# Adding the halves of y in the store, two queues for the last results, and a later place for two loads

## The chip, the cores and the metric

The kernel runs on one core of a Trainium2 chip. What counts is the device time of one execution in microseconds (us); the text compares medians of several runs. The core has five engines that work side by side: TensorE (PE in the rows, its weight loads PEld), VectorE (DVE), ScalarE (ACT), GpSimd (POOL) and SyncE (SP). SP, ACT and POOL can each issue DMA transfers; every one of them issues in the order of its own instructions, so an issue that waits holds up what stands behind it on that engine.

## What is computed

Local attention (chunks of 32 queries over 64 keys) gives x of 3072 x 512. Two gated blocks without activation follow:

```python
a = x @ w1 ; b = x @ w2            # 512 -> 1024
y = ((a * b) @ w3) @ w_out         # 1024 -> 1024 -> 512
a = y @ w_a ; b = y @ w_b          # 512 -> 1536
out = (a * b) @ w_out2             # 1536 -> 512
```

All is float32; the kernel splits every float32 operand into a high and a low part and makes a product from three matrix multiplications.

## The kernel before

The tokens are cut into six blocks of 512 (`t` = 0 to 5, `TT` = 512, `NT1` = 6). The first four go through the first gated block one by one while attention still runs. Blocks 4 and 5 go through it as one pair, with seven block products in place of eight (`seven12`); all three pairs go through the second gated block that way (`seven`). One call of `seven` makes one of 12 gate blocks (`f` = 0 to 11) from 42 matrix multiplications of 512 columns. The loop over pairs is called a stage here: first stage (`si` = 0, blocks 0 and 1), second (`si` = 1, blocks 2 and 3), third (`si` = 2, blocks 4 and 5).

**The pair's y.** For blocks 4 and 5 the sum over the 1024 inner columns is made in two halves (`h` = 0, 1). In each half eight results (`groups`, 128 x 512 each) are copied from PSUM by ACT (`copied`, L1041) into a buffer `tmp` of eight, and SP stores them in HBM, the first half to `yh`, the second to `yd` (L1169). `y_sums` adds the two much later: in the second stage it loads both (L851), DVE adds them (L1479), and SP stores the sum to `yd` (L1480). `x_sums` then makes the differences of the next pair's y that the seven products want (`xm`).

**Weights of the gate blocks.** POOL loads each gate block's factors in two DMAs (`w7_a` L920 with 640 KB, `w7_b` L939 with 256 KB) into two buffers in turn. ACT makes their high parts (`w7_hi`, L107), DVE the low parts (L110), between the copies and sums that `seven` does for PE. The factors used in call `f` are loaded in call `f` - 2 and split in call `f` - 1.

**Where the first stage begins**, several things meet: the last stores of y, the raw output weights of the last two blocks `j` = 4, 5 (`o_late`: four DMAs of 512 KB into the region of `gh`, L1390), and the first factors of the output products (`fo_load`: 768 KB each, L1209). `o_late` is a generator whose steps `hooks` calls at fixed places (`f`, `n`) of the loop; `n` counts four points inside one `seven`.

**Results.** `out_put` subtracts or adds on DVE (L1363), transposes on DVE (L1364), and issues four stores of 64 KB per piece on SP (L1367). `owed` holds four `out_put` calls of a stage that are done in the next stage at places (`f`, `n`).

Of the kernel before, what the change touches and what calls it, by code (L numbers as in the profile page):

```python
# [11 lines left out]
ALU = mybir.AluOpType  # L12

P = 128
# [9 lines left out]
TT = 512  # L24
# [23 lines left out]
def tile_attention_moe(  # L48
# [32 lines left out]
    def dram_tile(n, shape):  # L81
        return dram.tile(shape, F32, name=n, tag=n)

    yd = [dram_tile(f"yd{i}", [P, KD, TT]) for i in range(NT1)]
    yh = {i: dram_tile(f"yh{i}", [P, KD, TT]) for i in range(ND, NT1)}
    xd = {i: dram_tile(f"xd{i}", [P, KD, TT]) for i in range(ND, NT1)}

    W7 = 7 * CH // 2
# [1034 lines left out]
    for t in range(ND, NT1, 2):  # L1123
        for h in range(2):
            gs = {}
            held[:] = [psx.tile([P, 512], F32, tag="x", name="ps7")[:, :TT] for _ in range(2)]
            for m in range(HM * h, HM * h + HM):
                gs[m] = g_new(2 * (m % HM)), g_new(2 * (m % HM) + 1)
                if m == M1 - 1:
                    xn = []  # L1130
                    xg = x_build(xn, xd, t + 2) if t + 2 < NT1 else x_build(xn, yd, 0)
                    next(xg)
                seven12(m, w7.pop(0), *gs[m])
            if h == 1:
                while fo_rest:
                    fo_lo[0]()
                xn.extend(x_new() for _ in range(8))
                fo_hi[:] = [xn[7].rearrange("p l k t -> p (l k) t")]
            groups = [(n, i) for n in range(KD) for i in range(2)]
            ps_of = {}  # L1140

            def y_some(j, m0, m1):
                n, i = groups[j]
                if j not in ps_of:
                    ps_of[j] = psd.tile([P, 512], F32, tag="d", name="psY")
                for m in range(HM * h + m0, HM * h + m1):
                    for k, (a, b) in enumerate(PASSES):
                        mm(
                            ps_of[j][:, :TT],
                            wsm[m][:, a, P * n : P * n + P],  # L1150
                            gs[m][i][:, b, :],
                            m % HM == 0 and k == 0,
                            m % HM == HM - 1 and k == 2,
                        )

            for j, (n, i) in enumerate(groups):
                if j == 0:
                    y_some(0, 0, HM - 1)
                    sixth()
                    g_split()  # L1160
                    if h == 1:
                        w7_split(2)
                        w7_ab()
                    y_some(1, 0, HM - 1)
                    y_some(2, 0, HM - 1)
                y_some(j, HM - 1 if j < 3 else 0, HM)
                ps = ps_of.pop(j)[:, :TT]
                z = copied(ps)
                nc.sync.dma_start(out=(yd if h else yh)[t + i][:, n, :], in_=z)  # L1169
                if h == 1:  # L1170
                    for _ in range(2 + (j > 0)):
                        next(xg, None)
                    hook(4)
                else:
                    hook()
        for _ in xg:
            pass
        xs = xn
# [174 lines left out]
    def out_new(pool, tag):  # L1353
        return [pool.tile([P, 512], F32, tag=tag, name="ops") for _ in range(2)]

    def out_put(ps, y, op, t, n, banks=(0, 1), dst=None):
        for b in banks:
            if dst is None:
                sb = tmp()
                ob = cp.tile([P, TT], F32, tag="ob", bufs=3, name="ob")  # L1360
            else:
                sb, ob = gated(0, HF + dst + b), gated(1, HF + dst + b)
            nc.vector.tensor_tensor(sb, ps[b], y[b], op)  # L1363
            nc.vector.transpose(ob, sb)  # L1364
            for i in range(4):
                c0 = HC * n + P * b + SQ * i
                (nc.sync, nc.sync, nc.sync, nc.sync)[i].dma_start(  # L1367
                    out=out[t * TT : t * TT + TT, c0 : c0 + SQ].rearrange("(s p) c -> p s c", p=SQ),
                    in_=ob[SQ * i : SQ * i + SQ].rearrange("p (s c) -> p s c", c=SQ),
                )  # L1370

    def kept(ps, z):
        for b in range(2):
            nc.scalar.activation(z[b], ps[b], AF.Copy)
        return z

    def chain(*gs):
        for g in gs:
            yield from g

    def o_late():
        n = CH // 2
# [44 lines left out]
                nc.vector.tensor_tensor(x, x, e.bitcast(F32), ALU.subtract)  # L1427
                store(j, k, 1, x)

        for j in js[:2]:  # L1430
            for i in range(2):
                load(j, i)
        yield
        for j in js:
            for i in range(2):
                for _ in conv(j, i):
                    yield
            if j + 2 < HF:
                for i in range(2):
                    load(j + 2, i)  # L1440
            a, b = ((0, 2), (6, 8))[j - JE]
            sums[j] = [u[:, a + i // 2, n * (i % 2) : n * (i % 2) + n] for i in range(4)]
            s2 = [u[:, a + i] for i in range(2)]
            free[:] = [b, b + 1] + free[:2]
            for x in ((0, 1), (2, 3)):
                for i in x:
                    add(j, i)
                yield
            for k, x in ((0, decs[j, 0]), (2, s2[0]), (4, s2[1]), (6, decs[j, 1][:, :n])):
                hi(j, k, x)  # L1450
                yield
                lo()
# [3 lines left out]
    def room(i):  # L1456
        return [spare[:, 2 * i + b] for b in range(2)]

    def y_sums():
        todo = [(n, i) for n in range(KD) for i in range(ND, NT1)]  # L1460
        pend = []

        def load():
            if todo:
                n, i = todo.pop(0)
                k = 2 * (len(todo) % 2)
                x, y = spare[:, k], spare[:, k + 1]
                y_load(x, yd, i, n)
                y_load(y, yh, i, n)
                pend.append((n, i, x, y))  # L1470

        load()
        yield
        while pend:
            load()
            for _ in range(4):
                yield
            n, i, x, y = pend.pop(0)
            nc.vector.tensor_tensor(x, x, y, ALU.add)  # L1479
            nc.sync.dma_start(out=yd[i][:, n, :], in_=x)  # L1480
            yield

    def other(n):
        for _ in range(n):
            next(cw, None)
# [3 lines left out]
    for si, t in enumerate(seq):  # L1489
        nxt = seq[si + 1] if si + 1 < len(seq) else None  # L1490
        if si == 0:
            spare = spare_of(xs.pop())
            cw = x_sums(nxt)
            ow = o_late() if JE < HF else iter(())
            next(ow, None)
        elif si == 1:
            cw = chain(y_sums(), x_sums(nxt))
        order = (B11, T1, T2, B22, T3) if nxt is not None or not 1 else (B11, T1, T2, T3, B22)
        todo = [(i, j) for i in order for j in range(HF)]
        pd = pb = None  # L1500
        for f in range(M2):
            j = f - HF
            if si == 0 and f in (2, 3, 7, 8):
                fo_load(1, nc.sync)

            def hooks(n):
                if n == 0 and j >= 0:
                    put(T4, j, nc.vector)
                    put(B21, j, nc.vector)
                if owed and (f, n) in ((0, 1), (0, 2), (0, 3), (1, 0), (1, 1), (1, 2)):  # L1510
                    out_put(*owed.pop(0))
                if n > 0 and f == M2 - 1:
                    for _ in range((0, 1, 2, 2)[n]):
                        put(*todo.pop(0), nc.vector)
                if si == 0:
                    for _ in range((1, 0, 1, 2)[n] if f in (1, 2, 3, 4, 5) else 0):
                        next(ow, None)
                other((1, 0, 1, 1)[n] * (f >= 6) if si == 0 else (2 * (f > 0), 0, 2, 1)[n])

            if si == 0 and f == HF:  # L1520
                for _ in ow:
                    pass
            seven(w7.pop(0), gated(0, f), gated(1, f), hooks)
            if j >= 0:
                if j == 0:
                    pd, pb = out_new(pso, "o"), out_new(pso, "o")
                out_part(t, pd, T4, j, True)
                s_sum(1, j)
                s_sum(3, j)
                out_part(t, pb, B21, j, True)  # L1530
# [9 lines left out]
        for i in order:  # L1540
# [13 lines left out]
                    out_part(t, ps, i, j, i in (B11, T1))  # L1554
                step += 1
            if final and i == B22:
                out_put(pa, p4, ALU.subtract, t, 0, dst=2)
                out_put(pa, s5, ALU.add, t, 1, dst=4)
            if final:
                for b in range(2):  # L1560
                    for j in range(HF):
                        out_part(t, ps, i, j, False, (b,), b == 1)
                    if i == B22:
                        out_put(pc, u2, ALU.add, t + 1, 1, (b,))
                        continue
                    out_put(pa, p4, ALU.subtract, t, 0, (b,))
                    out_put(pa, s5, ALU.add, t, 1, (b,))
# [103 lines left out]
```

## Time and profile before

| What | us |
|---|---|
| median of 3 runs (1037.01 to 1041.54) | 1040.45 |
| the profiled execution, its own time | 1042.75 |
| its span in the trace | 1040.9 |
| PE busy | 1023.6 (98%) |
| DVE busy | 733.4 (70%) |
| ACT busy | 491.2 (47%) |
| POOL busy | 155.3 (15%) |

The profiled execution took 1.85 us more than its span, and it was longer than each of the three runs. Busy PE is not PE at its best, since matrix multiplications overlap and since the granted clock can be below full speed. All times in the rows below count from the span's start.

### The profile page before, as it was taken

What the parts mean: (1) busy time and instruction counts of PE and PEld (TensorE: products, weight loads), DVE (VectorE), ACT (ScalarE), POOL (GpSimd) and SP (SyncE); (2) the same over time, 40 slices, a digit from 0 to 9 for tenths busy, and PEclk for the clock granted to TensorE, in tenths of its full rate; (3) what the DMA queues carried; (4) which work ended last, traced back from release to release, by engine and by line L of the source; (5) the groups of instructions that cost most, each with busy time, mean ns of one, the idle gap of its engine ahead of it and who ended that gap; (6) DMA issues with size and microseconds to landing.
All of it is one profiled execution on the core that took longest, in us unless ns stands there. A gap on an engine that the chain in (4) does not pass through costs nothing.

```text
span 1040.9 us, 18743 instructions
## 1 busy us (share of the span) xinstructions
PE 1023.6 (98%) x7294; PEld 816.9 (78%) x7294; DVE 733.4 (70%) x1166; ACT 491.2 (47%) x883; POOL 155.3 (15%) x204
## 2 busy tenths in 40 slices
PE   9899999999999999999999999999999999999996
PEld 3458888888888888888878888877888888888885
DVE  4888936666665356768767778986677996666694
ACT  5676613444443345465545335643433653343342
POOL 0111497122232000001001000001011000100000
PEclk9999999999999999999999999999999999999999
DMA  8886567768886434577645774987538787223174
GB/s 330 295 238 195 156 205 241 236 230 275 276 298 190 133 106 162 175 271 230 220 155 180 244 246 145 315 238 201 184 118 273 258 304 189 91 87 132 36 219 104
DMA packets 147800, 212.95 MB, mean 205 GB/s; under 512 B 60544, under 2 KB 101376, under 8 KB 146432
## 3 DMA queue, kind: packets, MB, share of 16 engines
q1 hardware_dynamic: 137104, 170.30, 50.6%
q0 software_dynamic: 9856, 40.38, 12.0%
q8 instruction: 57, 0.93, 0.4%
q10 hardware_dynamic: 752, 1.09, 0.3%
q14 instruction: 31, 0.25, 0.1%
HBM read 159.29 MB, written 52.43 MB: 203 GB/s over the span
## 4 chain that ended last, share of the span: by engine, by line
PE 41%; DVE 5%; issue 4%; DMA 3%; ACT 1%; SPq 0%; DVEq 0%; POOLq 0%; ACTq 0%
PE ps L1029 28%; PE ops L1327 12%; DMA w<-wc 2%; DVE wo L1218 1%; DMA x<-yh 1%; DVE w L110 0%; DVE x L110 0%; DVE tmp L1278 0%; DMA x<-yd 0%; DVE ob L1364 0%; DVE gl L1349 0%; DVE tmp L1363 0%; DVE tmp L1045 0%; ACT wo L107 0%; DVE gh L1363 0%
## 5 line engine op out<-in xcount | busy, mean ns | idle before, releaser
L1029 PE MATMUL ps<-x,w 128*128 128x512 f32 x1848 | 427.1, 391 | 4.0 <-ACT tmp L1041 2.4
L1029 PEld LDWEIGHTS ps<-x,w 128*128 128x128 f32 x1848 | 346.4, 188 | 81.4 <-ACT tmp L1041 3.9
L1041 ACT ACTIVATE tmp<-ps 128x512 f32<-128x512 f32 x132 | 78.6, 595 | 248.8 <-PE ps L1029 195.8
L1327 PE MATMUL ops<-wo,fo 128*128 128x512 f32 x756 | 174.9, 390 | 0.2 <-DVE wo L1218 0.2
L1327 PEld LDWEIGHTS ops<-wo,fo 128*128 128x128 f32 x756 | 141.7, 188 | 30.5 <-DVE wo L1218 0.8
L110 DVE TENSOR_TENSOR w<-w 128x512 fp32r<-128x512 f32 (+1 forms) x176 | 105.5, 619 | 42.8 <-ACT w L107 42.7
L97 PE MATMUL psY<-g,wo 128*128 128x512 f32 x576 | 134.5, 392 | 0.0
L97 PEld LDWEIGHTS psY<-g,wo 128*128 128x128 f32 x576 | 107.4, 188 | 22.3
L1278 DVE TENSOR_TENSOR tmp<-ps,tmp 128x512 f32<-128x512 f32 x108 | 74.2, 687 | 33.2 <-PE ps L1029 30.6
L97 PE MATMUL psA<-xt,w 128*128 128x512 f32 x384 | 94.4, 395 | 0.5 <-ACT xt L107 0.5
L107 ACT ACTIVATE w<-w 128x512 fp32r<-128x512 f32 (+1 forms) x176 | 92.1, 571 | 3.8 <-DMA w<-wc 3.8
L97 PE MATMUL psB<-xt,w 128*128 128x512 f32 x384 | 93.8, 393 | 0.0
L97 PEld LDWEIGHTS psA<-xt,w 128*128 128x128 f32 x384 | 70.8, 188 | 15.7 <-ACT xt L107 0.9
L97 PEld LDWEIGHTS psB<-xt,w 128*128 128x128 f32 x384 | 71.2, 188 | 14.9
L920 POOL DMA_DIRECT2D w<-wc x36 | 19.3, 536 | 418.1 <-PE ps L1029 177.2
L1218 DVE TENSOR_TENSOR wo<-gl,wo 128x512 fp32r<-128x512 f32 x90 | 59.7, 686 | 28.8 <-ACT wo L107 28.8
L412 ACT ACTIVATE raw<-raw 128x512 f32<-128x512 f32 (+1 forms) x62 | 46.2, 745 | 32.1 <-DMA raw<-in_wab 17.5
L107 ACT ACTIVATE wo<-gl 128x512 fp32r<-128x512 f32 x90 | 52.9, 626 | 9.3 <-PE ops L1327 8.9
L97 PE MATMUL wps<-w_f 128*128 128x512 f32 x112 | 50.3, 599 | 0.6 <-DVE w_f L418 0.6
L413 ACT ACTIVATE raw<-raw 128x512 uint32<-128x512 uint32 (+1 forms) x62 | 46.2, 745 | 0.0
L762 DVE TENSOR_TENSOR gv<-psB,gv 128x512 f32<-128x512 f32 x32 | 22.0, 687 | 28.1 <-PE psB L97 24.4
L97 PEld LDWEIGHTS wps<-w_f 128*128 128x128 f32 x112 | 20.6, 190 | 25.6 <-issue 21.3
(103 smaller groups left out, 1010.0 us busy)
## 6 DMA issues: line engine op xcount, KB each, us to landing
fo<-fo SPq DMA_DIRECT2D x42, 768.0 KB
w<-wc POOLq DMA_DIRECT2D x36, 640.0 KB, 4.4
raw<-in_wab SPq DMA_DIRECT2D x24, 512.0 KB
v<-in_vw SPq DMA_DIRECT2D x64, 168.0 KB
w<-wc POOLq DMA_DIRECT2D x36, 256.0 KB, 4.7
kraw<-in_kt SPq DMA_DIRECT2D x16, 512.0 KB
raw<-in_w3a SPq DMA_DIRECT2D x6, 1024.0 KB
q<-in_qt SPq DMA_DIRECT2D x16, 384.0 KB
```

The costliest lines, as they stand in the source:

```text
L97: nc.tensor.matmul(o, lhsT=l, rhs=r, start=first, stop=last)
L107: nc.scalar.activation(hi, src, AF.Copy)
L110: nc.vector.tensor_tensor(lo, src, hi.bitcast(F32), ALU.subtract)
L412: nc.scalar.activation(h, h, AF.Prelu, scale=2.0**-112, alpha=2.0**32)
L413: nc.scalar.activation(l, l, AF.Copy, scale=2.0**-29)
L762: nc.vector.tensor_tensor(gv, psB[:, :TT], gv, ALU.mult)
L920: nc.gpsimd.dma_start(out=t[:, 1, :C7].bitcast(F32), in_=wseq[n][:, :C7])
L1029: nc.tensor.matmul(ps, lhsT=w[i][:, a, k, :], rhs=xs[i][:, b, k, :], start=first and n == 0, stop=n == 5, skip_group_check=not first,)
L1041: nc.scalar.activation(z, ps, AF.Copy)
L1218: low.tensor_tensor(e[:, 1, :n], src, e[:, 0, :n].bitcast(F32), ALU.subtract)
L1278: nc.vector.tensor_tensor(z, ps, y, ALU.add)
L1327: nc.tensor.matmul(ps[s], lhsT=w[:, b, P * s : P * s + P], rhs=e[:, a, :], start=fresh and j == 0 and n == 0, stop=j == HF - 1 and n == 2, ...
```

## The change

Five edits. The second half of y is no longer stored by SP to an array of its own: POOL stores it with addition onto the first half, and `yh` and `y_sums` are gone. `x_sums` of the second stage starts at `f` = 5 alone. `o_late` asks for the raw weights of `j` = 5 after it has converted those of `j` = 4, and the first two `fo_load` move from `f` = 2, 3 to `f` = 3, 5. The four `owed` results go to places (0,1), (0,3), (1,1), (1,3). The stores of the last stage's results are dealt to SP and ACT in turn (`late`).

```diff
-    yh = {i: dram_tile(f"yh{i}", [P, KD, TT]) for i in range(ND, NT1)}
...
-                nc.sync.dma_start(out=(yd if h else yh)[t + i][:, n, :], in_=z)
+                if h == 0:
+                    nc.sync.dma_start(out=yd[t + i][:, n, :], in_=z)
+                else:
+                    nc.gpsimd.dma_start(out=yd[t + i][:, n, :], in_=z, accum_op=ALU.add)
...
-    def out_put(ps, y, op, t, n, banks=(0, 1), dst=None):
+    def out_put(ps, y, op, t, n, banks=(0, 1), dst=None, late=False):
...
-                (nc.sync, nc.sync, nc.sync, nc.sync)[i].dma_start(
+                ((nc.sync, nc.scalar, nc.sync, nc.scalar) if late else (nc.sync, nc.sync, nc.sync, nc.sync))[i].dma_start(
...
-        for j in js[:2]:
+        for j in js[:1]:
             for i in range(2):
                 load(j, i)
         yield
...
-            if j + 2 < HF:
+            if j + 1 < HF:
                 for i in range(2):
-                    load(j + 2, i)
+                    load(j + 1, i)
...
-    def y_sums():
-        todo = [(n, i) for n in range(KD) for i in range(ND, NT1)]
...
         elif si == 1:
-            cw = chain(y_sums(), x_sums(nxt))
+            cw = x_sums(nxt)
...
-            if si == 0 and f in (2, 3, 7, 8):
+            if si == 0 and f in (3, 5, 7, 8):
                 fo_load(1, nc.sync)
...
-                if owed and (f, n) in ((0, 1), (0, 2), (0, 3), (1, 0), (1, 1), (1, 2)):
+                if owed and (f, n) in ((0, 1), (0, 3), (1, 1), (1, 3)):
                     out_put(*owed.pop(0))
...
-                other((1, 0, 1, 1)[n] * (f >= 6) if si == 0 else (2 * (f > 0), 0, 2, 1)[n])
+                other((1, 0, 1, 1)[n] * (f >= 6) if si == 0 else (1, 0, 1, 1)[n] * (f >= 5))
...
-                out_put(pa, p4, ALU.subtract, t, 0, dst=2)
-                out_put(pa, s5, ALU.add, t, 1, dst=4)
+                out_put(pa, p4, ALU.subtract, t, 0, dst=2, late=True)
+                out_put(pa, s5, ALU.add, t, 1, dst=4, late=True)
...
-                        out_put(pc, u2, ALU.add, t + 1, 1, (b,))
+                        out_put(pc, u2, ALU.add, t + 1, 1, (b,), late=True)
```

On SP, where the first gated block ends and the first stage begins, the queue stood like this before; `yd_84`, `yd_85` are blocks 4 and 5 of y (the last two of eight stores), `gh<-in_w2o` the raw loads, `fo_102`, `fo_103` (`fo_100`, `fo_101` after the change) the prepared output weights in HBM:

```order
L1169 DMA yd_84<-tmp 128x512
L1169 DMA yd_85<-tmp 128x512
L1390 DMA gh<-in_w2o 128x1024 x4
L1209 DMA fo<-fo_102 128x1536
L1412 DMA fo_103<-gh 128x2x256 x3
L1209 DMA fo<-fo_102 128x1536
L1412 DMA fo_103<-gh 128x2x256 x3
L1412 DMA fo_103<-gh 128x256 x2
```

After the change SP's queue has at the same place (`xb<-yd_80` and `xb<-yd_81` load blocks 0 and 1 of y, and stood between the y stores before):

```order
L850 DMA xb<-yd_80 128x512 x2
L850 DMA xb<-yd_81 128x512 x2
L1388 DMA gh<-in_w2o 128x1024 x4
L1410 DMA fo_101<-gh 128x2x256 x3
L1211 DMA fo<-fo_100 128x1536
L1410 DMA fo_101<-gh 128x2x256 x3
L1410 DMA fo_101<-gh 128x256 x2
L1211 DMA fo<-fo_100 128x1536
```

The eight stores of y have left the queue, the four raw loads still stand one behind the other, and the first factor load has moved from right behind them to behind the first three stores of converted weights, the second to behind five more.

On POOL, after the change, the queue at the end of the first gated block (`wc_88` is the first gate block's factors, `wc_90` the third's):

```order
L919 DMA w_4047<-wc_88 128x1280
L938 DMA w_4047<-wc_88 128x512
L919 DMA w_4571<-wc_89 128x1280
L938 DMA w_4571<-wc_89 128x512
L1171 DMA yd_84<-tmp 128x512
L1171 DMA yd_85<-tmp 128x512
...
L1171 DMA yd_85<-tmp 128x512
L919 DMA w_4047<-wc_90 128x1280
L938 DMA w_4047<-wc_90 128x512
```

Before, the load of the third block's factors stood directly behind the second's; now eight adding stores are ahead of it on the same engine.

On DVE, at the start of the second stage, before (`ps` are the products in PSUM, L1363 and L1364 the owed results, L1479 the addition of y):

```order
L1363 TENSOR_TENSOR gh<-gh,x_5404 128x512
L1364 STREAM_TRANSPOSE gh<-gh 128x512
L1278 TENSOR_TENSOR tmp<-ps_7161,tmp 128x512
L110 TENSOR_TENSOR w_4049<-w_4049 128x512 x2
L1278 TENSOR_TENSOR tmp<-ps_7160,tmp 128x512
L110 TENSOR_TENSOR w_4049<-w_4049 128x256
L1479 TENSOR_TENSOR x_7068<-x_7068 128x512
L1278 TENSOR_TENSOR tmp<-ps_7196,tmp 128x512
```

And the same stretch after the change:

```order
L1366 STREAM_TRANSPOSE gh<-gh 128x512
L109 TENSOR_TENSOR w_4047<-w_4047 128x512 x2
L1280 TENSOR_TENSOR tmp<-ps_7148,tmp 128x512
L109 TENSOR_TENSOR w_4047<-w_4047 128x256
L1280 TENSOR_TENSOR tmp<-ps_7184,tmp 128x512
```

The addition between the low parts of the factors and the sum that `seven` makes from its next product is gone, as are the other seven like it.

## Rows read from the trace of the kernel before

**Rows 1.** The page's first part: busy time, share of span, instructions.

```profile
PE 1023.6 (98%) x7294; PEld 816.9 (78%) x7294; DVE 733.4 (70%) x1166; ACT 491.2 (47%) x883; POOL 155.3 (15%) x204
```

**Rows 2.** Timeline of PE alone: start, us, instructions, [idle before <- releaser].

```profile
509.88 16.57 PE L1029 MATMUL ps<-x,w 128*128 128x512 f32 x72
528.57 49.75 PE L1029 MATMUL ps<-x,w 128*128 128x512 f32 x210 [2.12 <-ACT tmp L1041]
578.60 3.02 PE L1029 MATMUL ps<-x,w 128*128 128x512 f32 x12 [0.28 <-ACT tmp L1041]
...
686.72 21.75 PE L1029 MATMUL ps<-x,w 128*128 128x512 f32 x94
709.68 46.15 PE L1029 MATMUL ps<-x,w 128*128 128x512 f32 x200 [1.21 <-DVE w L110]
...
860.68 67.20 PE L1029 MATMUL ps<-x,w 128*128 128x512 f32 x294
```

**Rows 3.** Stretches: us, PE busy, granted clock, DMA share, GB/s.

```profile
509.50:510.50 1.00, 1.00 (x6) 1.00 0.70 262
512.00:518.00 6.00, 6.00 (x28) 1.00 1.05 277
518.00:525.00 7.00, 7.00 (x33) 1.00 0.99 399
528.00:534.00 6.00, 5.43 (x17) 0.72 0.25 74
708.00:710.00 2.00, 0.79 (x4) 1.00 0.97 331
1033.00:1039.00 6.00, 0.00 (x0) 0.93 0.70 120
```

**Rows 4.** Timeline of all engines where the first stage begins.

```profile
508.86 2.49 DVE L110 TENSOR_TENSOR x<-xb,x 128x512 fp32r<-128x512 f32 x4
...
510.35 1.56 ACT L1041 ACTIVATE tmp<-psY 128x512 f32<-128x512 f32 x3
...
512.44 1.92 SPq L1390 DMA_DIRECT2D gh<-in_w2o  x4
...
514.40 0.51 SPq L1209 DMA_DIRECT2D fo<-fo  x1
...
518.66 0.53 POOL L920 DMA_DIRECT2D w<-wc  x1 [27.39 <-PE ps L1029]
...
526.88 1.15 ACT L107 ACTIVATE w<-w 128x512 fp32r<-128x512 f32 x2 [2.47 <-DMA w<-wc]
```

**Rows 5.** DMA issues: name, queue, count, size, median us to landing.

```profile
w<-wc POOLq DMA_DIRECT2D x36, 640.0 KB, 4.4
```

**Rows 6.** SP's own timeline, the second factor load of the first stage.

```profile
546.31 0.49 SPq L1209 DMA_DIRECT2D fo<-fo  x1
```

**Rows 7.** Timeline of all engines early in the second stage.

```profile
700.94 0.43 SPq L851 DMA_DIRECT2D x<-yh  x1
...
706.54 0.69 DVE L1479 TENSOR_TENSOR x<-x 128x512 f32<-128x512 f32 x1 [1.92 <-DMA x<-yh]
...
708.95 0.69 DVE L110 TENSOR_TENSOR w<-w 128x512 fp32r<-128x512 f32 x1
```

**Rows 8.** Timeline of all engines at the end of the span.

```profile
1025.57 8.56 SPq L1367 DMA_DIRECT2D out<-gh  x16
...
1033.67 0.71 DVE L1364 STREAM_TRANSPOSE ob<-tmp 128x512 f32<-128x512 f32 x1
1034.23 4.27 SPq L1367 DMA_DIRECT2D out<-ob  x8
```

**Rows 9.** One line of the kernel on two queues: issue ns min/median/max.

```profile
L1226 SPq DMA_DIRECT2D x<-yd x6: 529/570/632, 602.1 to 796.9; - x6
L1226 ACTq DMA_DIRECT2D x<-yd x2: 590/736/881, 572.9 to 573.5; - x2
```

More of the change, by code (lines that the diff above doesn't have):

```diff
@@ L1375, in kept @@
         return z
-    def chain(*gs):
-        for g in gs:
-            yield from g
     def o_late():
@@ L1457, in room @@
         return [spare[:, 2 * i + b] for b in range(2)]
-    def y_sums():
-        todo = [(n, i) for n in range(KD) for i in range(ND, NT1)]
[L1461 to L1481, printed above, removed]
     def other(n):
```

## The prediction

> **What bounds the kernel now.** I read the page first: PE is busy for 98% of the span [rows 1], so an edit counts only where PE waits, where its clock is below full speed, or after its last instruction. The timeline of PE alone then shows where that is, because the three stages hold the same work: 294 matrix multiplications of L1029 before the first output product. In the third stage these took 67.20 us without a gap. In the second they ran from 686.72 to 709.68 + 46.15 = 755.83, which is 69.11 us, and in the first from 509.88 to 578.60 + 3.02 = 581.62, which is 71.74 us [rows 2]. So the second stage loses 1.91 us and the first 4.54 us against the third. The third place is the tail: after the last transpose on DVE the span goes on for 6.5 us [rows 8].
>
> In the first stage PE stood for 2.12 us before 528.57 and for 0.28 us before 578.60 [rows 2], and in the 6 us from 528 the granted clock averaged 0.72 [rows 3], worth 0.28 x 6 = 1.7 us: right after the longer gap the clock was at its lower level for a while, 1.2 instead of 2.4 GHz. What ended the gap is in the timeline of all engines: ACT waited 2.47 us for the third gate block's factors [rows 4], and the copy that PE needed stood behind that wait on ACT. That load was issued at 518.66 and used at 526.88, 8.2 us later [rows 4]; the median of its kind is 4.4 us [rows 5]. Ahead of it SP had issued, from 512.44, four raw loads of 512 KB and one factor load of 768 KB [rows 4], and the DMA engines were full from 512 to 525, with 277 GB/s at first and 399 GB/s after 518 [rows 3].
>
> In the second stage PE stood for 1.21 us before 709.68 [rows 2], with the clock at 1.00 throughout [rows 3]. DVE had stood 1.92 us in the addition of y, waiting for the second half's load, which SP had issued at 700.94; the low parts that PE wanted (L110, 708.95) were queued behind it on DVE [rows 7].
>
> **The change part by part.** I work from the profiled execution, whose own time is 1042.75 us, 1.85 us above its span. It lies 2.30 us above the median of the three runs. I carry the sum in us over to that median, since a median is what will be measured.
>
> *No y_sums.* Sixteen loads, eight additions of about 0.69 us on DVE [rows 7] and eight stores disappear. DVE is not the bound on average, so only the place where PE waited counts: 1.21 us certainly, and with the loads that crowded the next factor loads gone probably the rest of the 1.91. Against that, x_sums now starts at f = 5, with two loads of 512 KB beside a factor load. The first stage has the same two loads just before its output products, and lost 0.28 us there [rows 2]. So -1.91 + 0.28 = -1.6 us; bounds -0.9 (only 1.21 comes back, 0.28 is lost) and -1.9. The owed results keep their work on DVE and move apart by one point: nothing, as the third stage shows that a stage with owed results can run without a gap [rows 2].
>
> *Raw loads in two parts.* This does less than its words. On SP nothing that waits stands between the loads of j = 4 and of j = 5; in the order of the change they are one row of four. They write different parts of a buffer that is already free, so they go out back to back as before. I give this edit nothing. Their start can move: they were behind the eight y stores, the last of which needed the ACT copies that ended at 510.35 + 1.56 = 511.91, and went out at 512.44. Now they are held only by the buffers, whose last DVE reader ended at 508.86 + 2.49 = 511.35 [rows 4]. So 0 to 1.1 us earlier; I take 0.5.
>
> *The first factor load later.* It leaves the crowd, 786,432 bytes at 399 GB/s, so 2.0 us less ahead of the gate factors. It now goes out where the second did, at 546.31 [rows 6], and the second follows five stores later. Their consumers start at 581.62, some 30 us after; with a landing like that of the 640 KB loads (4.4 us) nothing waits.
>
> *Adding stores on POOL.* Eight plain stores of 256 KB on SP become eight adding ones on POOL. POOL had nothing to issue for 27.39 us here [rows 4], so its issue time is covered. ACT made the last three copies in one burst before 511.91, hence three of these stores arrive just before the raw loads, and a fourth shortly before that; the gate factors of 518.66 then follow on the same queue. The trace holds no adding store. From below it costs as much as a plain one: one such store alone had the DMA engines for 1 us with 262 GB/s, busy for 0.70 of it [rows 3]. From above it is that plus one more load and one more store of 256 KB, 0.66 us (at 399 GB/s) and about 1 us. I take one more load, 0.66 us each or 2.0 us for three, since the old sum has to be fetched once and the write is the plain store's. Bounds: 0 and 5.0 us.
>
> The Trainium skill says of an addition inside the DMA engines (Collectives: The Full Stack, section "The bandwidth ceiling: the fold count and why AG ≠ RS ≠ AR") that it needs two source reads, which double the reading side; no row here shows one. By that rule the extra is one read of 256 KB, the value taken above.
>
> Sum for the gate factors' landing: -2.0 - 0.5 + 2.0 = -0.5 us; bounds -2.0 - 1.1 = -3.1 and +3.0. PE's gap of 2.12 us then shrinks to 1.6. The clock did not fall after 1.21 us of gap and did after 2.12 us; between them I count half of the 1.7 us. First stage: -0.5 - 0.85 = -1.35 us. From -3.8 (gap and clock loss both gone) to +3.0.
>
> *Two queues at the end.* SP issued the last 24 stores one after the other, 8.56 / 16 = 0.535 us each, and its last issue ended at 1034.23 + 4.27 = 1038.50, although the last transpose was done at 1033.67 + 0.71 = 1034.38 [rows 8]; the span ended 2.4 us after the last issue. Transposes come every 1.3 us, four stores each, two per queue in 1.07 us: both queues keep up. After 1034.38 there are two issues left on each, 1035.45, and with 2.4 us behind, 1037.85. That is 3.05 us less. For the same line an issue on ACT took 590 and 881 ns against at most 632 on SP [rows 9]; two of them at 0.2 us more each make it 2.65 us, rounded to -2.6. Bounds: -3.05 and 0.
>
> The Trainium skill holds against this edit that DMAs issued from several engines run on the same 16 DMA engines, so that only sequencer time is saved, "usually small relative to the DMA itself" (DMA: Bandwidth & Descriptors, "Issuing engines are not separate DMA queues"). By that rule the edit is worth next to nothing if the DMA engines are the limit here. The row of this stretch has them busy for 0.70 of it at 120 GB/s [rows 3], so there is room: 24 stores x 0.535 x 0.70 = 9.0 us of full DMA time, and from the first issue at 1025.57 that ends at about 1034.6, before the last issue of the sum above.
>
> Total: -1.6 - 1.35 - 2.6 = -5.55 us, 1037.2 us for an execution like the profiled one, and 1040.45 - 5.5 = **1035.0 us** for the median.
>
> **The rivals.**
>
> *The gap in the first stage closes.* If the addition costs no more than the store, the factors land 2.0 to 3.1 us earlier and PE gets its 2.12 + 1.7 us back: -3.8 in place of -1.35, so 1032.5 us. For it speaks that the four adding stores begin before the raw loads, while the DMA engines had room at 509.5 (0.70 busy) [rows 3].
>
> *The gap grows.* With 1.66 us extra per addition the landing is 5.0 - 2.5 = 2.5 us later, the gap 4.6 us and the clock loss stays: +2.5 - 1.6 - 2.6 = -1.7, so 1038.7 us. For it speaks that this stretch is full already [rows 3].
>
> *The tail stays.* If the small stores can't go faster than 120 GB/s whatever the queue, 2.6 us are missing: 1037.6 us. Against it speaks the 0.70.
>
> *Slower: POOL's queue backs up.* The factors stand behind the adding stores on one queue. Four of these from about 509, each taking d, end at 509 + 4d; beyond d = 2.4 us the factors of 518.66 start late. The other parts give 4.2 us, so the whole is even when the landing is 4.2 us later than now, at 531.1, which with 4.4 us of landing means a start at 526.7, d = 4.4 us. It is 0.5% slower from d = 5.7 us. A single load here took 700.94 to 706.54 = 5.6 us from issue to use [rows 7], so additions done strictly one after the other, each with a full landing, would reach that. At d = 6.5 the factors land at 539.4, 12.5 us later than now: +12.5 - 4.2 = +8.3, so 1048.8 us. Against it: a plain store of this size had the DMA engines for about 1 us [rows 3], and 5.7 us is more than five times that.
>
> **How the numbers follow.** Chances: the sum as worked out 0.45 (1033 to 1037.5), gap closed 0.20, gap grown 0.15, tail stays 0.12, slower 0.08. A measurement of this kernel can tell about 0.5%, 5.2 us, from no change: the line is 1035.2. The forecast lies on it, so half of its chance counts as faster, and nearly all of the closed gap: 0.23 + 0.19 + about 0.04 of the rest = 0.46. Slower by over 0.5% is the queue that backs up, 0.08. Within it lies the remaining 0.46. The range runs from 1031.0 (all terms at their better bounds: -3.8 - 1.9 - 3.05 = -8.75, 1031.7, less a little for the spread of the runs) to 1040.0, which takes in the grown gap and the tail that stays, and leaves out the slower case.
>
> **What would show it.** In the timeline of PE the first stage's 294 multiplications end some 1.4 us sooner after their start, with a gap of 1 to 2 us ended by ACT, and the second stage's take 67.3 to 68 us with no wait on DVE. ACT's wait for the gate factors shows their landing. The four raw loads still stand together on SP, from about 511.5. At the end SP and ACT each issue 12 stores, and the span ends about 4 us after the last transpose. The prediction is wrong if the adding stores take over 2.4 us each, if the third gate block's factors land later than 8.2 us after their issue, or if DMA's busy share at the end stays at 0.70 with two queues.

## The result, and the profile after

The changed kernel took 1052.61 us (median of 5 runs, 1050.85 to 1054.64), the kernel before 1039.13 us beside it (5 runs). The ratio is 1.0129, 95% interval 1.0104 to 1.0153: slower by 13 us, where 5.5 us less was forecast. The profiled execution was the shortest of its five (1050.85 us, span 1049.1 us), and the one before was longer than all five of its runs, so the two traces differ by only 8.2 us.

The timeline of PE shows where they went:

```profile
508.54 6.96 PE L1028 MATMUL ps<-x,w 128*128 128x512 f32 x30
518.29 2.93 PE L1028 MATMUL ps<-x,w 128*128 128x512 f32 x6 [2.80 <-ACT tmp L1040]
522.83 6.79 PE L1028 MATMUL ps<-x,w 128*128 128x512 f32 x18 [1.61 <-DVE tmp L1280]
531.36 3.06 PE L1028 MATMUL ps<-x,w 128*128 128x512 f32 x12 [1.74 <-ACT tmp L1040]
536.27 1.66 PE L1028 MATMUL ps<-x,w 128*128 128x512 f32 x6 [1.86 <-ACT tmp L1040]
539.53 28.94 PE L1028 MATMUL ps<-x,w 128*128 128x512 f32 x126 [1.60 <-ACT tmp L1040]
569.15 19.43 PE L1028 MATMUL ps<-x,w 128*128 128x512 f32 x84 [0.68 <-ACT tmp L1040]
589.01 3.02 PE L1028 MATMUL ps<-x,w 128*128 128x512 f32 x12 [0.42 <-ACT tmp L1040]
...
698.42 66.99 PE L1028 MATMUL ps<-x,w 128*128 128x512 f32 x294
...
871.55 66.99 PE L1028 MATMUL ps<-x,w 128*128 128x512 f32 x294
```

The first stage's 294 multiplications now take 589.01 + 3.02 - 508.54 = 83.49 us against 71.74 [rows 2]: 11.75 us more. The other pieces, after less before, each from one row's start to the next: up to the first stage 508.54 - 509.88 = -1.34; the first stage's output products 1.29 more (592.03 to 698.42, before 581.62 to 686.72); the second stage's 294 multiplications 66.99 - 69.11 = -2.12; its output products 1.29 more (765.41 to 871.55, before 755.83 to 860.68); from the third stage to the end of the span 177.55 - 180.22 = -2.67. Together 8.20 us.

The first stage has seven waits instead of two. The windows of it (us, PE busy, granted clock, DMA share, GB/s):

```profile
512.00:518.00 6.00, 3.50 (x16) 0.96 1.02 315
518.00:522.00 4.00, 2.93 (x6) 0.50 0.63 131
522.00:526.00 4.00, 3.17 (x8) 0.50 0.46 66
526.00:530.00 4.00, 3.61 (x12) 0.78 0.43 65
530.00:536.00 6.00, 3.06 (x12) 1.00 0.56 104
```

The waits add up to 10.7 us against 2.4 before, 8.3 more. After the first wait of 2.80 us the clock is at its lower level for eight microseconds and more. The six multiplications from 518.29 took 2.93 us there, and six at the full clock took 1.66 (the row of 536.27). The eighteen from 522.83 took 6.79 us; at the full clock I estimate 4.4, from 66.99 / 294 = 0.228 us each and the 0.29 us that the row of six lies above that. So the clock costs 3.7 us, against about 1.7 before: 2.0 more. The rest, 1.4 us, fits the work being cut into eight pieces in place of three, at 0.29 us a piece (an estimate too). From 518 on the DMA engines are about half idle, so it is no lack of transfer rate.

POOL's timeline, from the second of the eight adding stores on, shows what they wait for (the bracket is POOL's idle time and what ended it; "issue" is time in which the engine waited for nothing that the profile shows):

```profile
499.76 0.89 POOL L1171 DMA_DIRECT2D yd<-tmp  x1 [3.97 <-ACT x L106]
505.58 0.88 POOL L1171 DMA_DIRECT2D yd<-tmp  x1 [4.92 <-issue]
509.94 0.87 POOL L1171 DMA_DIRECT2D yd<-tmp  x1 [3.48 <-ACT tmp L1040]
517.85 0.87 POOL L1171 DMA_DIRECT2D yd<-tmp  x1 [7.04 <-issue]
522.27 0.87 POOL L1171 DMA_DIRECT2D yd<-tmp  x1 [3.55 <-issue]
526.55 0.88 POOL L1171 DMA_DIRECT2D yd<-tmp  x1 [3.41 <-issue]
530.91 0.88 POOL L1171 DMA_DIRECT2D yd<-tmp  x1 [3.48 <-issue]
531.52 0.84 POOL L919 DMA_DIRECT2D w<-wc  x1
535.82 0.56 POOL L938 DMA_DIRECT2D w<-wc  x1 [3.46 <-issue]
```

The last four stores stand (530.91 - 517.85) / 3 = 4.35 us apart, although their data lay ready: ACT made its last copies of y by 508.84 + 1.56 = 510.40 (the first of its rows below). The view of the tile `yd` gives how long the eight stores took from issue to landing (until the data had arrived in HBM):

```profile
DMA to landing us min/median/max: 4.0/4.3/7.6
```

Distance and landing are the same: one adding store is under way at a time. The third gate block's factors, behind them, are issued at 531.52 instead of 518.66 [rows 4]. But ACT's timeline shows that they come last in the matter:

```profile
508.84 1.56 ACT L1040 ACTIVATE tmp<-psY 128x512 f32<-128x512 f32 x3
...
517.64 0.60 ACT L1040 ACTIVATE tmp<-ps 128x512 f32<-128x512 f32 x1 [3.14 <-DMA yd<-tmp]
...
530.71 0.60 ACT L1040 ACTIVATE tmp<-ps 128x512 f32<-128x512 f32 x1 [11.64 <-DMA yd<-tmp]
...
535.62 0.60 ACT L1040 ACTIVATE tmp<-ps 128x512 f32<-128x512 f32 x1 [3.21 <-DMA yd<-tmp]
537.84 1.15 ACT L106 ACTIVATE w<-w 128x512 fp32r<-128x512 f32 x2 [1.63 <-DMA w<-wc]
```

Each store keeps one of the eight `tmp` buffers until it has landed. ACT and DVE copy and sum the first stage's products into the same buffers, so they wait for the stores (18.0 us for ACT alone, in three waits), PE waits for them, and the factors are waited for by 1.63 us at the end.

At the end of the span the timeline of all engines has

```profile
1036.23 4.86 SPq L1369 DMA_DIRECT2D out<-gh  x8
1036.24 5.30 ACTq L1369 DMA_DIRECT2D out<-gh  x8
...
1042.06 3.86 SPq L1369 DMA_DIRECT2D out<-ob  x4
1042.32 3.69 ACTq L1369 DMA_DIRECT2D out<-ob  x4
...
1044.34 0.71 DVE L1366 STREAM_TRANSPOSE ob<-tmp 128x512 f32<-128x512 f32 x1
```

From the end of the last transpose, 1045.05, to the end of the span it is 4.05 us, against 6.5 before [rows 8].

### The profile page after: what moved, and what is told of

Read it like the earlier page. It is cut to its first block, busy times and chain, and to the rows that moved or that the text cites. A ratio compares the mean times of both kernels' runs of the same rounds, so it can differ in the third digit from the quotient of the medians.

```text
span 1049.1 us, 18690 instructions
## 1 busy us (share of the span) xinstructions
PE 1026.9 (98%) x7294; PEld 816.7 (78%) x7294; DVE 731.7 (70%) x1158; ACT 491.9 (47%) x883; POOL 162.6 (15%) x212
## 4 chain that ended last, share of the span: by engine, by line
PE 41%; DVE 4%; issue 4%; DMA 3%; ACT 1%; POOL 1%; SPq 0%; POOLq 0%; ACTq 0%; DVEq 0%
PE ps L1028 30%; PE ops L1329 11%; DVE wo L1220 1%; DMA w<-wc 1%; DMA x<-yd 1%; DVE x L109 1%; POOL yd L1171 1%; DVE ob L1366 0%; ACT wo L106 0%; DVE tmp L1365 0%; DMA fo<-cs 0%; DVE gl L1351 0%; ACT x L1376 0%; DVE tmp L1044 0%; SPq L1369 0%
```

## The experiments

The ratio is always to the kernel before, run beside on the same chip; its medians were 1039.77 us for the first four kernels, 1040.32 for the next four, 1040.21 for the last two.

| Run | Edit | us, median | ratio, 95% interval |
|---|---|---|---|
| e1 | changed kernel, 1024 bytes for POOL's transfers | 1038.97 | 0.9988, 0.9978 to 0.9999 |
| e2 | changed kernel, stores on POOL without addition | 1035.24 | 0.9955, 0.9941 to 0.9968 |
| e3 | changed kernel, y and its sums as before | 1034.71 | 0.9951, 0.9937 to 0.9965 |
| e4 | kernel before, two queues at the end | 1036.86 | 0.9968, 0.9955 to 0.9980 |
| e5 | changed kernel, third factors on SP | 1050.10 | 1.0107, 1.0088 to 1.0126 |
| e6 | kernel before, two factor loads later | 1038.59 | 0.9985, 0.9976 to 0.9993 |
| e7 | changed kernel, sum on DVE in place of the adding store | 1040.75 | 0.9999, 0.9987 to 1.0011 |
| e8 | e7, x_sums from f = 1 | 1041.49 | 1.0011, 1.0000 to 1.0022 |
| e9 | changed kernel, 768 bytes | 1039.68 | 1.0000, 0.9985 to 1.0014 |
| e10 | kernel before, 1024 bytes | 1040.04 | 0.9998, 0.9982 to 1.0013 |

**e1, more room.** Both kernels set aside 512 bytes of each partition for the descriptors of POOL's transfers (`dynamic_dma_scratch_size`). The theory: one adding store fills more than half of that, and the next waits until it has landed.

```diff
-        "TRN2", target_bir_lowering=False, num_devices=1, dynamic_dma_scratch_size=512
+        "TRN2", target_bir_lowering=False, num_devices=1, dynamic_dma_scratch_size=1024
```

> The changed kernel with 1024 in place of 512 bytes per partition for the descriptors of POOL's DMAs, nothing else. Theory A (room): an adding store fills so much of the 512 bytes that the next one is issued only when it has landed, so the eight go one at a time, 4.3 us each. Then with 1024 bytes two or three are in flight, the burst of three is issued within about 3 us, PE's 11.7 us loss in the first stage shrinks to 5 us or less, and the time is 1038 to 1046 us. Theory B (slow addition): the DMA engines themselves need 4.3 us for each addition, whatever is queued. Then the stores are issued sooner but land no sooner, the last still about 20 us after the copies, and the time stays at 1050 to 1054 us.

It took 1038.97 us: this one number gives back the whole loss against the kernel before. POOL's timeline:

```profile
510.88 0.87 POOL L1171 DMA_DIRECT2D yd<-tmp  x1 [7.23 <-ACT tmp L1040]
512.93 1.75 POOL L1171 DMA_DIRECT2D yd<-tmp  x2 [1.17 <-ACT tmp L1040]
515.34 0.86 POOL L1171 DMA_DIRECT2D yd<-tmp  x1 [0.66 <-DVE tmp L1280]
520.13 0.57 POOL L919 DMA_DIRECT2D w<-wc  x1 [3.93 <-PE ps L1028]
```

No wait is called "issue" any more; the stores go out as ACT makes the results, two of them (from 512.93) in one piece. The Trainium skill says of transfers issued by GpSimd that their descriptors are written to rings in a part of SBUF and drained from there (DMA: Bandwidth & Descriptors, "SWDGE vs HWDGE vs iDMA"). The runs fit this and add that the issuing engine waits where that part is too small; here the stores then went out 4.35 us apart.

**e2, no addition.** The second half is stored plainly, so the first half is missing from blocks 4 and 5 of y.

```diff
-                    nc.gpsimd.dma_start(out=yd[t + i][:, n, :], in_=z, accum_op=ALU.add)
+                    nc.gpsimd.dma_start(out=yd[t + i][:, n, :], in_=z)
```

> The changed kernel, its second half of y stored by POOL without the addition; this leaves the sum of the two halves out, so the result lacks the first half for blocks 4 and 5. Theory A and theory B both expect plain stores of 256 KB to go out about 1 us apart, as the factor loads do, and the first stage to lose 2 to 4.5 us: 1034 to 1038 us. Rival C (POOL's queue): any store there, added or not, waits for the one before. Then the stores are again over 3 us apart and the time stays near 1050.

1035.24 us. Moving the stores to POOL is harmless; the addition is what costs. With the same 512 bytes three plain stores go out in one piece:

```profile
510.91 1.78 POOL L1171 DMA_DIRECT2D yd<-tmp  x3 [1.49 <-ACT tmp L1040]
518.18 0.55 POOL L919 DMA_DIRECT2D w<-wc  x1 [5.49 <-PE ps L1028]
```

Against e1 there are 3.7 us between (intervals apart): what the addition costs when there is room. In e1 PE still waited 2.9 us for ACT's `tmp` in the first stage (1.2 us in e2), and landing took 6.9 us in the median, 4.2 us in e2.

**e3, the sums as before.** `yh`, `y_sums` and the places of `owed` and `x_sums` of the kernel before; the later factor loads, the raw loads in two parts and the two queues stay.

```diff
-                if h == 0:
-                    nc.sync.dma_start(out=yd[t + i][:, n, :], in_=z)
-                else:
-                    nc.gpsimd.dma_start(out=yd[t + i][:, n, :], in_=z, accum_op=ALU.add)
+                nc.sync.dma_start(out=(yd if h else yh)[t + i][:, n, :], in_=z)
...
-            cw = x_sums(nxt)
+            cw = chain(y_sums(), x_sums(nxt))
```

> The changed kernel with the addition undone: yh, y_sums and the places of the owed results as before; the later first factor load, the loop over j and the two queues at the end stay. If all of the loss comes from the adding stores, this is the kernel before less 2.5 us at the end and less up to 2 us in the first stage for the later factor load: 1034.5 to 1037 us. If part of the loss comes from the later loads, it is above 1039.

1034.71 us, the fastest of all and 0.5% below the kernel before. It does the separate sums that e2 leaves out, and takes no longer. In its timeline of PE the wait in the second stage, 1.21 us before [rows 2], is 0.26 us:

```profile
703.70 45.88 PE L1029 MATMUL ps<-x,w 128*128 128x512 f32 x200 [0.26 <-DVE w L110]
```

**e4, two queues alone**, on the kernel before:

```diff
-                (nc.sync, nc.sync, nc.sync, nc.sync)[i].dma_start(
+                ((nc.sync, nc.scalar, nc.sync, nc.scalar) if late else (nc.sync, nc.sync, nc.sync, nc.sync))[i].dma_start(
```

> The kernel before with the last stage's result stores dealt to SP and ACT, nothing else. The trace after the change has 5.5 us from PE's last instruction to the end of the span, before it was 8.0; so -2.5 us, 1036.5 us, ratio 0.9976. If the stores were limited by the DMA engines, no change.

1036.86 us, 2.9 us less.

**e5, the factors taken out of POOL's queue.** It tells the two paths apart, held buffers and late factors:

```diff
-        nc.gpsimd.dma_start(
+        (nc.sync if n == NW3 else nc.gpsimd).dma_start(
```

> The changed kernel, with the third gate block's two factor loads issued by SP in place of POOL, so that they no longer stand behind the adding stores. Theory A (the stores that go one at a time hold the eight buffers tmp, and that alone stops ACT, DVE and PE): the waits for tmp stay, only the wait for the factors at the end goes, about 1.6 us of PE and a little clock; 1049 to 1052 us, first stage 80 to 83 us for its 294 multiplications. Theory B (the late factors are the cost, as the prediction's slower case had it): most of the 11.7 us of the first stage come back; 1040 to 1043 us.

1050.10 us: as theory A has it, though the first stage's 294 multiplications took 590.51 + 3.06 - 509.62 = 83.95 us, still more than the 80 to 83 expected. SP issued the loads at 520.04 and 525.80 (two of the four raw loads came behind them, at 526.17), and ACT, which needs the factors only later (at 539.18, without a wait), stood for the buffers all the same:

```profile
534.26 0.60 ACT L1041 ACTIVATE tmp<-ps 128x512 f32<-128x512 f32 x1 [15.15 <-DMA yd<-tmp]
```

**e6, the later factor loads alone**, on the kernel before:

```diff
-            if si == 0 and f in (2, 3, 7, 8):
+            if si == 0 and f in (3, 5, 7, 8):
```

> The kernel before with one edit, the first two factor loads of the output products at f = 3, 5 in place of 2, 3. If that edit carries what the third run gained over the fourth (1034.71 against 1036.86 us, 2.15 us): 1037.5 us, ratio 0.998, PE's gap near 527 us gone or under 0.5 us. If the raw loads in two parts carried it: no difference, ratio 1.000, gap still about 2 us.

1038.59 us, ratio 0.9985; less than was expected, but faster. PE's gap of 2.12 us is gone, and with it the stretch at the lower clock; the first 198 multiplications run through:

```profile
509.93 45.20 PE L1029 MATMUL ps<-x,w 128*128 128x512 f32 x198
555.67 19.34 PE L1029 MATMUL ps<-x,w 128*128 128x512 f32 x84 [0.54 <-ACT tmp L1041]
575.39 3.02 PE L1029 MATMUL ps<-x,w 128*128 128x512 f32 x12 [0.37 <-ACT tmp L1041]
```

The executions of e4 and e10, which keep the two loads early, show the gap too, but not the lower clock. This is e4, PE's row behind the gap and the window around it (us, PE busy, granted clock, DMA share, GB/s):

```profile
527.23 48.11 PE L1029 MATMUL ps<-x,w 128*128 128x512 f32 x210 [1.89 <-ACT tmp L1041]
...
526.00:530.00 4.00, 2.77 (x12) 1.00 0.00 0
```

The ratio of e3 to e4, 0.9951 / 0.9968 = 0.9983, is this edit and the raw loads in two parts together; so nothing is left for the raw loads that these runs can tell.

**e7, the addition on DVE while y is made.** The first half is loaded again into `tmp`, three results ahead:

```diff
+                    z = first.pop(0)
+                    onto(z, ps, z, ALU.add)
+                    if j + 3 < len(groups):
+                        first.append(y_load(tmp(), yh, t + groups[j + 3][1], groups[j + 3][0]))
+                nc.sync.dma_start(out=(yd if h else yh)[t + i][:, n, :], in_=z)
```

> The changed kernel without adding stores: the first half of y is loaded again while the second is made, DVE adds it to the product straight from PSUM (in place of ACT's copy), SP stores the sum; no separate sums in the second stage. Eight loads of 256 KB come back, ACT loses eight copies, DVE gets eight additions of 0.69 us. If adding early is as good an idea as having no later sums, and only the adding store was bad: 1033.5 to 1036 us, ratio 0.994 to 0.997, at or below the plain stores on POOL (1035.24) . If the loads beside the last products hold up the raw loads and the factors: above 1037 us, with PE's gap in the first stage over 2 us.

1040.75 us: the better guess fell. The second stage has no wait (66.99 us for its 294), but the last products of y and the start of the first stage have:

```profile
509.49 3.01 PE L97 MATMUL psY<-g,wo 128*128 128x512 f32 x12 [2.38 <-DVE tmp L1045]
513.79 1.63 PE L1029 MATMUL ps<-x,w 128*128 128x512 f32 x6 [1.29 <-DVE tmp L1045]
```

The first stage begins at 513.79, some 5 us later than in e3 (508.72). Its own gaps, 1.29 and 0.69 us, are no gap of over 2 us, so the other guess does not describe the loss either. The trace suggests that SP's queue delays the first stage's inputs: the loads of `xb` stand there behind stores that wait for DVE's additions, and go out from 500.88 (495.70 in the changed kernel). The addition that ended the 2.38 us ran on DVE at 508.75, right behind work on `xb` that had come late. No run tests this.

**e8, x_sums earlier**, on e7, to explain the 1.29 us that the changed kernel loses in the second stage's output products:

```diff
-                other((1, 0, 1, 1)[n] * (f >= 6) if si == 0 else (1, 0, 1, 1)[n] * (f >= 5))
+                other((1, 0, 1, 1)[n] * (f >= 6) if si == 0 else (1, 0, 1, 1)[n] * (f >= 1))
```

> As the run before, but the differences for the third pair (x_sums of the second stage) start at f = 1 in place of f = 5. In the traces of the changed kernel, with 1024 bytes, and with plain stores, PE lost 0.9 to 1.4 us in the output products of the second stage, and none where the separate sums stood ahead of x_sums. If the late place of x_sums makes that loss: 1 us less than the run before, and the time from the end of the second stage's 294 multiplications to the third stage's first is 104.9 us, not 106.0 to 106.6. If not: the same time within 0.5 us and still 106 us or more.

1041.49 us, no gain, and 105.62 us from the end of the 294 to the third stage (756.66 to 862.28). Besides, e7 with the late place took 104.57 us there (754.68 to 859.25), less than any other. So the late place of x_sums alone does not make the loss.

**e9 and e10, the room again.** 768 bytes in the changed kernel, 1024 in the kernel before, by the line that e1 shows.

> The changed kernel with 768 bytes per partition set aside for the descriptors of POOL's transfers, between the 512 that it has and the 1024 of the first run. If one adding store takes more than half of 768, still only one can be under way: spacing of the stores 4.3 us as at 512, 1050 to 1054 us. If it takes less than that, two can be under way and the time is nearly that of 1024 (1038.97): 1038 to 1042 us, spacing about 2.2 us or as ACT makes the results.

> The kernel before with 1024 bytes in place of 512, nothing else. If the room matters only to the adding stores: no difference, ratio 0.998 to 1.002. If plain loads on POOL waited for room too, or the larger share of the buffer memory costs something: a ratio outside of that, and the first run's gain would not be the adding stores' alone.

e9 took 1039.68 us: with 768 bytes two adding stores can be under way, and only the last two wait for room, behind the burst of ACT's copies:

```profile
514.16 0.87 POOL L1171 DMA_DIRECT2D yd<-tmp  x1 [1.48 <-issue]
520.11 0.88 POOL L1171 DMA_DIRECT2D yd<-tmp  x1 [5.07 <-issue]
```

e10 took 1040.04 us, ratio 0.9998: without adding stores the room makes no difference.

## Why the prediction was wrong

**Adding stores on POOL: the step that failed.** "I take one more load, 0.66 us each" priced the addition by the time that it has the DMA engines. What it has is 4.35 us of POOL's queue each, since the 512 bytes let the next one go only when the one before has landed. The term was +2.0 us with an upper bound of 5.0; against e2 the changed kernel stands 1.0129 / 0.9955 = 1.0175, or 18 us, worse. e1 splits this: 1.0129 / 0.9988, 14.6 us, is the room, and 0.9988 / 0.9955, 3.4 us (3.7 by the medians), the addition itself.

The slower rival named the mechanism (stores strictly one after the other, each with a full landing), with a chance of 0.08. It was put aside because a plain store "had the DMA engines for about 1 us". That is the wrong one of two durations: the time from issue to landing is the other, and for loads the rows had it (4.4 us for 640 KB in [rows 5], 5.6 us to use in [rows 7]). At d = 4.4 us, which is nearly what was measured, the rival then said "even", and that was wrong in two ways. Five stores, not four, went out from 509.94 on, since the earlier ones were late already (505.58, after 4.92 us of "issue"), and one of them took 7.9 us beside the raw loads, so the factors were 12.9 us late, not 8. And it priced only the factors. The other path, `tmp` held until a store lands, was not in the text; by e5 it holds PE up even when the factors are on another queue.

Of the prediction's three signs of being wrong one came: the stores stood 4.35 us apart. The third gate block's factors were in use 6.3 us after their issue (531.52 to 537.84), for it was the issue that came late. And the DMA engines' share at the end did not stay at 0.70: with two queues they were full, at 152 GB/s (share 1.08, 1036 to 1042).

**No y_sums.** Forecast -1.6 us, "67.3 to 68 us with no wait on DVE": 66.99 us, -2.12. Right in its place, but no gain for the whole: e3, which keeps the sums, is as fast as e2. The wait of 1.21 us on which the term rested was 0.26, 0.31 and 0.42 us in e3, e6 and e10, and absent in e4: it was large in the one execution that I had. And the changed kernel gave 1.29 us back in the second stage's output products, where the sum had 0.28. PE's waits there, for `fo` and `wo`, differ between kernels (none in e3, 0.37 us in e6, 1.43 us in e2); what sets them stays open, since e8 did not show it. The 1.29 us in the first stage's output products are open as well.

**Raw loads in two parts.** Nothing, as forecast; they stay four in one row, now from 509.91. That is 2.5 us earlier instead of 0.5, but 1.34 us of it is that the whole stage began earlier; the other 1.2 us lie near the upper bound of 1.1.

**The first factor load later.** The direction was right, the size too small: 2.0 us less ahead of the factors was thought to leave 1.6 us of the gap. Alone (e6) it removes the gap and the clock loss, and the first stage takes 575.39 + 3.02 - 509.93 = 68.48 us instead of 71.74. In the median 0.15% is left of it, 1.6 us. The profiled execution of the kernel before had a slow first stage: in e4 and e10, which keep these loads early, it took 575.49 + 3.02 - 508.83 = 69.68 us and 576.66 + 3.02 - 509.35 = 70.33 us, with gaps of 1.89 and 1.67 us; against those e6 gains 1.2 and 1.9 us. The granted clock stayed at 1.00 behind both. So the 1.7 us of clock that the prediction counted on, by half, belonged to one execution, as the 1.21 us did.

**Two queues at the end.** Forecast -2.6 us; 6.5 - 4.05 = 2.45 in the traces, 2.9 us by e4's medians. The last issue ended 0.96 us after the last transpose (1042.06 + 3.86 = 1045.92 on SP, 1042.32 + 3.69 = 1046.01 on ACT), near the 1.07 of the sum, and 3.1 us lay behind it instead of 2.4. So the size is right in part by luck: the 0.4 us that the sum added for slower issues on ACT stand where 0.7 us more behind the last issue came. The rule of the Trainium skill that was weighed there (DMA: Bandwidth & Descriptors, "Issuing engines are not separate DMA queues": issuing from several engines saves only sequencer time, usually little) describes it. But here that time was not little: before, SP alone issued the eight stores from 1034.23 on in 4.27 us, and the last transpose was done at 1034.38 [rows 8].

The best version that came of it is e3: the two edits that work, without the adding store.

## What to carry to other kernels

A transfer that no row shows can have three prices, and here the smallest was the time that it has the DMA engines: ask also how long it takes from issue to landing, and what has to wait for the landing (the buffer that it reads, the next transfer of its kind). The adding stores from GpSimd needed more of the memory set aside for its transfers than plain ones of the same size; the lack of it looked like a run of waits called "issue", with the issues a landing apart. A wait of a microsecond in a single execution, or the lower clock behind one, is not yet a term: see whether a second execution has it.

## What was not expected of the hardware

- A 128 x 512 float32 adding store occupied POOL 0.87 us per issue, a plain one 0.54 us (e2). With 512 bytes per partition set aside, one adding store at a time was under way, but three plain ones in one piece; with 768 and 1024 bytes the time fell from 1052.6 to 1039.7 and 1039.0 us.
- One at a time, the adding stores landed in 4.3 us (median of the changed kernel, the fastest 4.0). The plain ones of e2 took 4.2 us in the median although three went out together, and the fastest 2.6. Where several adding stores were under way, it was 6.9 us (e1).
- Among the last stores of the changed kernel, an issue from `gh` took 0.316 us on SP and 0.384 us on ACT (medians of 8 each), in e3 0.408 and 0.386. The prediction had ACT 0.2 us slower, by [rows 9]. SP alone took 0.494 us in the kernel before (median of 16).
